# Unit 2's transposed k by a transposing transfer, its state products eight matmul rows later

## The chip, the cores and the metric

The kernel runs on one core of a Trainium2 chip. The metric is the device time of one execution in microseconds (us); the figure given for a kernel is the median of its runs. Profiles come from one profiled execution, whose times run from the start of its span.

## What is computed

Two blocks follow one another, on 4 batches of 768 tokens. The first is a gated linear recurrence in 8 heads of 48 columns, the second a normalization and a two-layer network of width 384 and 1536 with a residual:

```python
f = 1.0 / (1.0 + np.exp(-f_logit))
for t in range(S):
    state = f[:, :, t, :, None] * state + np.einsum('bhd,bhe->bhde', k[:, :, t], v[:, :, t])
    y[:, :, t] = np.einsum('bhd,bhde->bhe', q[:, :, t], state)
...
xn = (x - mu) / np.sqrt(var + 1e-06) * g_ln
ch = np.maximum(xn @ w_ch1, 0.0) @ w_ch2
return (x + ch).astype(np.float32)
```

Data type is float32 throughout.

## The kernel before

The 768 tokens are cut into 12 units of 64 tokens of all 4 batches (256 rows each). Within a unit the recurrence is done by matmuls: gates and their running products (two scans, `after` and `upto`, on VectorE) scale k and q into `kh` and `qh`; `scores` multiplies them, `causal` masks the result into `sc`, `values` multiplies it by v into `py`, and `carried` adds what the state of earlier units gives. For the state that goes on to the next unit, kh is needed with tokens across partitions: the stage `kt` makes this transposed copy, `chunk` multiplies it by v into the PSUM tile `shared` (TensorE, line 851), and `state` adds it to `kept`, the state already scaled by the unit's gates. `stats`, `norm` and `turn` prepare the result for the network (mlp), whose steps are the tokens m0, m1 and so on. `x0`, `x1` are finished output rows of units 0 and 1, the tiles `po` their second-layer products.

Nothing is scheduled by a planner: the string START writes out by hand the order of the first units, UNIT that of one later unit, and each engine executes its instructions in the order in which they are recorded. Tokens: `a2.kt` is stage kt of unit 2; `m0` a step of unit 0's network; `l4k` a load (capital L on ACT's queue); `u`, `U`, `t`, `T` mix weights on VectorE or GpSimd.

There are two ways to transpose. Units 0 to 2 use TensorE against an identity (tiles `tr`, `kp`) and copy the result out of PSUM. From unit 3 on (DIRECT = 3) a token pair such as P4k1 P4k0 first copies two halves of the 32-bit data as 16-bit planes (`split`: a ScalarE copy into a tile `planes`, of which there are three in rotation, then a DMA to DRAM, on SP's queue for a capital P and on GpSimd's for a small p), and a token such as x4k, or the stage kt, reads them back by a transposing DMA on SP's queue (`transfer`, `transposed`). The name K (tiles `Kplanes`, `Khalves`) stands for kh, small k, q and f for raw inputs.

Each DMA started by SP or ACT takes one of eight semaphores in turn, and its issuing queue waits there until the DMA that held it before has landed; in the rows of the order these are DMAHW0 to DMAHW7.

Of the kernel before, what the change touches and what calls it, by code (L numbers as in the profile page):

```python
# [306 lines left out]
h01 a1.upto w l1k h01 a1.kept f h01 h01 h00 a2.gates a1.q a1.kx a1.carried r l1v a1.k w f  # L307
a1.scores l3f a1.causal h00 r h01 a1.values a1.kt l2k f l2q w a1.stats r h01 a1.norm a1.rstd
a1.chunk P3f0 w h00 a1.turn a2.kx a2.after p3f1 a2.k r m1 m1 a2.upto f f l3k w a2.q r p3k0 x3f
a1.state m1 f a2.kept l4v P3k1 l2v m1 l3q r m1 m1 w x3k r a2.carried a3.gates w a2.scores w u U  # L310
a2.causal P3q1 m0 m0 a2.kt a3.after m0 U P3q0 L4f a2.values a3.k a2.stats L4k a2.chunk P4f1 m1
x3q m1 a2.state a3.upto p4f0 m0 l5f a2.norm U p3K1 u m0 a2.turn m0 P4k0 m1 P3K0 T a3.q x4f u u
P4k1 u a4.gates l4q u a3.kt a3.kept m2 m2 P5f0 m2 a3.carried l3v a4.after a3.scores m2 p4q0 x4k
m2 a4.upto u m2 u a3.causal p4q1 t m2 s2 a3.chunk a4.k t L5k a3.values a3.state x4q p5k0 a3.stats
m1 m1 a3.norm P5f1 P4K1 m2 U m2 a4.q x5f m2 p5k1 l6f l5q m2 a4.kept m2 a3.turn y3 l5v U m2 m1
p4K0 a5.gates
"""
UNIT = """
a{n}.kt a{n}.carried p{p}f1 a{o}.after a{n}.scores m{m} a{n}.causal m{m} m{m} m{m} P{o}q0 m{m}
# [8 lines left out]
def kernel(  # L328
# [22 lines left out]
    T = 64  # L351
# [9 lines left out]
    NU = S // T  # L361
# [3 lines left out]
    PLAIN = 2  # L365
    FIRST = 3
    DIRECT = 3
    HALVED = 1
    PIECE = 768
    R = 2  # L370
# [23 lines left out]
    def one_bank(name):  # L394
        return ps1.tile([P, 512], FP32, tag="one", name=name)
# [5 lines left out]
    for name in "fqk":  # L401
        t = consts.tile([P, G, H, 64], FP32, name=f"{name}raw")
# [11 lines left out]
    def raw_of(n, name):  # L414

        return wide_heads["k" if n >= DIRECT and name == "q" else name]

    by_gates = {}

    def split(n, name, i, queue):  # L420

        if n >= NU or n < DIRECT:
            return
        if (n, name) not in halved:
            halved[n, name] = drams.tile([P, 2, 2, 64 * H], U16, tag=f"{name}halves",
                                         name=f"{name}halves{n}")
        planes = raws.tile([P, 2, 64 * H], U16, tag="planes", bufs=3,
                           name=f"{name}planes{n}_{i}")
        if name == "K":
            src = by_gates[n].rearrange("p (i s) t -> p i (s t)", i=2)[:, i].bitcast(U16).rearrange(  # L430
                "p (c two) -> p two c", two=2)
            to, there = planes, halved[n, name][:, :, i]
        else:
            src = raw_of(n, name).rearrange("p g h e -> p (g h e)")[
                :, i * D:i * D + (H - 1) * R * D + 64]
            src = bass.AP(tensor=src.tensor, offset=src.offset,
                          ap=[src.ap[0], [R * D, H], [1, 64]]).bitcast(U16).rearrange(
                              "p h (c two) -> p two h c", two=2)
            to, there = planes.rearrange("p two (h c) -> p two h c", h=H), halved[n, name][:, i]
        nc.scalar.copy(out=to, in_=src)  # L440
        queue.dma_start(out=there, in_=planes)  # L441

    def transfer(n, name):

        if n >= NU or n < DIRECT:
            return
# [7 lines left out]
    def transposed(dst, blocks, there):  # L454
        nc.sync.dma_start_transpose(
            out=dst.bitcast(U16).rearrange("p (a r) -> p a r", a=blocks), in_=there)

    def load(n, name, gs=range(B // 2), engines=(nc.sync,)):
# [7 lines left out]
        for b in (b for b in range(B) if b // 2 in gs):  # L466
            to = loaded[n, name]
            if name == "v" or n < DIRECT:
                to = to[(b % 2) * T:(b % 2 + 1) * T, b // 2, :, 0:D]
# [166 lines left out]
    def attention(n):  # L636

        both = range(G)
        pairs, order = (by_batch, "g a") if n < DIRECT else (by_heads, "a g")
        gt = gates  # L640
# [5 lines left out]
        def new(name, shape, **kw):  # L646
            if name not in at:
                at[name] = work.tile(shape, FP32, tag=name, name=f"{name}{n}", **kw)
            return at[name]
# [35 lines left out]
        def times(dst, pts, by):  # L685
            for g, pt in pts.items():
                segs = segments([g])
                nc.vector.tensor_tensor(out=dst[:, segs], in0=pt, in1=by[:, segs, 1:E1],
                                        op=ALU.mult)

        def do_gates(gs=both):
            new("after", [P, NS, E1])
            new("upto", [P, NS, E1])
            new("total", [P, NS], bufs=2)
            if n >= DIRECT:
                nc.scalar.activation(out=gv[:, :, 1:E1], in_=turned["f"], func=AF.Sigmoid)
# [15 lines left out]
        def do_k(gs=both):  # L712
            kh = new("kh", [P, NS, T])
            if n < DIRECT:
                times(kh, {g: at["pk"][g] for g in gs}, at["after"])
            else:
                nc.vector.tensor_tensor(out=kh, in0=turned["k"], in1=at["after"][:, :, 1:E1],  # L717
                                        op=ALU.mult)
                by_gates[n] = kh

        def do_q(gs=both):
            qh = new("qh", [P, NS, T])
# [65 lines left out]
        def do_kt():  # L788

            kt, kh = new("kt", [P, GA, P]), at["kh"]  # L790
            if n >= DIRECT:
                transposed(kt.rearrange("p e c -> p (e c)"), GA,
                           halved.pop((n, "K")).rearrange("p two i c -> (p two) (i c)"))
                return
            for g in range(G):
                pt = one_bank(f"kp{n}").rearrange("p (a c) -> p a c", a=NP)
                for a in range(NP):
                    e = g * NP + a
                    nc.tensor.transpose(
                        pt[:, a], kh[:, 2 * e:2 * e + 2].rearrange("p b t -> p (b t)"), ident)  # L800
                nc.scalar.copy(out=kt[:, g * NP:(g + 1) * NP], in_=pt)
# [53 lines left out]
        def do_state():  # L855
            if n < NU - 1:
# [3 lines left out]
                else:  # L860
                    nc.scalar.copy(out=state, in_=pnv)

        stages = {"gates": do_gates, "after": do_after, "upto": do_upto, "kx": do_k_across,
                  "k": do_k, "q": do_q, "kept": do_kept, "carried": do_carried,
                  "scores": do_scores, "causal": do_causal, "kt": do_kt, "values": do_values,
                  "stats": do_stats, "rstd": do_rstd, "chunk": do_chunk, "state": do_state,
                  "norm": lambda gs=both: normalize(n, gs), "turn": lambda gs=both: turn(n, gs)}
        if n < HALVED:
            for name in ("gates", "after", "upto", "kx", "k", "q", "scores", "causal", "values",
# [5 lines left out]
    def normalize(n, gs):  # L875
        x = x_of[n]
        _, mv, rstd = norm_of[n]
        if n not in xn_of:
            xn_of[n] = work.tile([P, G, DM], FP32, tag="xn", name=f"xn{n}")
        for g in gs:  # L880
            if n < PLAIN:
                nc.vector.tensor_scalar(out=xn_of[n][:, g], in0=x[:, g], scalar1=mv[:, g, 0:1],
                                        scalar2=None, op0=ALU.subtract)
                continue
            nc.vector.tensor_scalar(out=xn_of[n][:, g], in0=x[:, g], scalar1=mv[:, g, 0:1],
                                    scalar2=rstd[:, g:g + 1], op0=ALU.subtract, op1=ALU.mult)

    def turn(n, gs):
        xn = xn_of[n]
        if n not in xt_of:  # L890
            xt_of[n] = work.tile([P, KD, W], FP32, tag="xt", bufs=2, name=f"xt{n}")
        xt = xt_of[n]
        for g in gs:
            pt = one_bank(f"xp{n}")[:, 0:KD * P].rearrange("p (m t) -> p m t", m=KD)
            for m in range(KD):
                nc.tensor.transpose(pt[:, m], xn[:, g, m * P:(m + 1) * P], ident)  # L896
            for m in range(KD):
                nc.scalar.mul(out=xt[:, m, g * P:(g + 1) * P], in_=pt[:, m],  # L898
                              mul=gain[:, m:m + 1])
# [117 lines left out]
    def mlp(n):  # L1017
# [6 lines left out]
        h = h_of[n]  # L1024
        if n < HALVED:
            pass
# [177 lines left out]
```

## Time and profile before

| | |
|---|---|
| median of 3 runs | 430.35 us (429.78 to 431.18) |
| the profiled execution's own time | 429.14 us |
| its span, first to last instruction | 427.4 us |
| TensorE matmul busy | 414.1 us, 97% of the span |
| VectorE / ScalarE / GpSimd busy | 331.6 / 214.4 / 123.4 us |
| mean granted TensorE clock | 0.988 |

The 1.74 us between own time and span lie before the first and after the last instruction. Where TensorE is busy without a break, the end is set by how much it has to do. The other engines' idle time then matters only where TensorE comes to wait for them.

### The profile page before, as it was taken

What the parts mean: (1) busy time and instruction counts of PE and PEld (TensorE: products, weight loads), DVE (VectorE), ACT (ScalarE), POOL (GpSimd) and SP (SyncE); (2) the same over time, 40 slices, a digit from 0 to 9 for tenths busy, and PEclk for the clock granted to TensorE, in tenths of its full rate; (3) what the DMA queues carried; (4) which work ended last, traced back from release to release, by engine and by line L of the source; (5) the groups of instructions that cost most, each with busy time, mean ns of one, the idle gap of its engine ahead of it and who ended that gap; (6) DMA issues with size and microseconds to landing.
All of it is one profiled execution on the core that took longest, in us unless ns stands there. A gap on an engine that the chain in (4) does not pass through costs nothing.

```text
span 427.4 us, 12961 instructions
## 1 busy us (share of the span) xinstructions
PE 414.1 (97%) x5429; PEld 386.6 (90%) x5429; DVE 331.6 (78%) x539; ACT 214.4 (50%) x364; POOL 123.4 (29%) x146
## 2 busy tenths in 40 slices
PE   6699999999999999999999999999999999999995
PEld 4589887667979999999999999999999999999995
DVE  5989896845986779879879879878879878664561
ACT  2495857452544464573574583573583453341320
POOL 2255543660033015016015016025025014012021
PEclk9599999999999999999999999999999999999999
DMA  9999999887989897886697897797695781301001
GB/s 171 286 223 183 216 281 229 190 206 182 177 121 233 164 226 207 209 192 176 166 235 186 192 220 173 184 213 201 161 221 154 178 130 50 88 2 28 13 9 34
DMA packets 167647, 71.68 MB, mean 168 GB/s; under 512 B 151760, under 2 KB 157840, under 8 KB 167584
## 3 DMA queue, kind: packets, MB, share of 16 engines
q1 hardware_dynamic: 151728, 54.38, 61.3%
q0 software_dynamic: 3872, 12.64, 8.4%
q10 hardware_dynamic: 11984, 3.79, 4.3%
q8 instruction: 44, 0.72, 0.7%
q14 instruction: 19, 0.16, 0.1%
HBM read 28.31 MB, written 23.59 MB: 121 GB/s over the span
## 4 chain that ended last, share of the span: by engine, by line
PE 90%; DVE 3%; DMA 2%; SPq 2%; ACT 2%; issue 1%; POOL 0%; ACTq 0%; DVEq 0%; POOLq 0%
PE pp L1062 32%; PE bx L961 11%; PE by L961 10%; PE po L1042 7%; PE ph L1032 7%; PE bz L961 4%; PE py L808 3%; PE py L758 3%; PE shared L772 2%; PE bw L961 2%; PE bv L961 2%; PE shared L851 2%; PE xp L896 2%; SPq L475 2%; DMA fraw<-in_f_logit_dram 1%; PE idle L577 1%
## 5 line engine op out<-in xcount | busy, mean ns | idle before, releaser
L972 ACT ACTIVATE h<-h 128x512 f32<-128x512 f32 x45 | 28.4, 631 | 44.0 <-DVE h L969 37.9
L1062 PE MATMUL pp<-mixed,h 128*128 128x192 f32 x240 | 42.4, 326 | 0.0
L1062 PE MATMUL pp<-w,h 128*128 128x192 f32 x240 | 40.8, 326 | 0.0
L1062 PE MATMUL pp<-mixed,s 128*128 128x192 f32 x240 | 40.6, 326 | 0.0
L1062 PEld LDWEIGHTS pp<-mixed,s 128*128 128x128 f32 x240 | 39.3, 190 | 0.0
L1062 PEld LDWEIGHTS pp<-w,h 128*128 128x128 f32 x240 | 38.9, 190 | 0.3
L1062 PEld LDWEIGHTS pp<-mixed,h 128*128 128x128 f32 x240 | 39.1, 190 | 0.1
L969 DVE TENSOR_TENSOR h<-h,bx 128x512 f32<-128x512 f32 x36 | 24.6, 683 | 16.9 <-PE bx L961 16.1
L898 ACT ACTIVATE xt<-xp,gain 128x128 f32<-128x128 f32 x72 | 20.0, 377 | 32.9 <-PE xp L896 32.9
L440 ACT COPY Kplanes<-kh 128x1024 uint16<-128x1024 uint16 x18 | 18.3, 1048 | 31.0 <-DVE kh L717 25.7
L441 POOL DMA_DIRECT2D qhalves<-qplanes x9 | 4.9, 548 | 97.5 <-ACT qplanes L440 97.5
L669 DVE TENSOR_TENSOR_SCAN after<-gates,ends 128x1040 f32<-128x1040 f32 (+1 forms) x13 | 28.1, 2165 | 6.2 <-ACT gates L700 3.4
L1032 PE MATMUL ph<-xt,w 128*128 128x256 f32 x144 | 31.9, 380 | 0.4 <-ACT xt L898 0.4
L1042 PE MATMUL po<-w,h 128*128 128x384 f32 x96 | 32.3, 489 | 0.0
L1032 PEld LDWEIGHTS ph<-xt,w 128*128 128x128 f32 x144 | 27.1, 190 | 4.5 <-ACT xt L898 0.6
L961 PE MATMUL bx<-y,v 128*128 128x128 f32 x216 | 28.5, 275 | 0.0
L681 DVE TENSOR_TENSOR_SCAN upto<-gates,starts 128x1040 f32<-128x1040 f32 (+1 forms) x13 | 28.1, 2158 | 0.5
L1042 PEld LDWEIGHTS po<-w,h 128*128 128x128 f32 x96 | 17.8, 190 | 11.3
L961 PEld LDWEIGHTS bx<-y,v 128*128 128x128 f32 x216 | 26.3, 192 | 0.0
L839 POOL TENSOR_SCALAR rstd<-mv 128x2 f32<-128x2 f32 x12 | 7.5, 626 | 61.4 <-DVE mv L832 61.3
L440 ACT COPY kplanes<-kraw 128x1024 uint16<-128x1024 uint16 x18 | 18.2, 1045 | 10.2 <-DMA kraw<-in_k_dram 6.7
L563 POOL TENSOR_TENSOR w<-w_0upper,w_0units 128x768 int32<-128x768 int32 x7 | 14.6, 2089 | 25.0 <-DVE w_0upper L561 20.7
(173 smaller groups left out, 961.7 us busy)
## 6 DMA issues: line engine op xcount, KB each, us to landing
w_0words<-in_moe_w_ch_dram SPq DMA_DIRECT2D x7, 768.0 KB, 6.3
v<-in_v_dram SPq DMA_DIRECT2D x46, 96.0 KB, 4.0
Khalves<-Kplanes POOLq DMA_DIRECT2D x16, 256.0 KB, 3.5
kraw<-in_k_dram SPq DMA_DIRECT2D x40, 96.0 KB, 4.1
fhalves<-fplanes POOLq DMA_DIRECT2D x14, 256.0 KB, 3.9
kraw<-in_q_dram SPq DMA_DIRECT2D x36, 96.0 KB, 3.0
fraw<-in_f_logit_dram ACTq DMA_DIRECT2D x27, 96.0 KB, 2.8
khalves<-kplanes POOLq DMA_DIRECT2D x9, 256.0 KB, 3.4
```

What stands on the lines that cost most here:

```text
L440: nc.scalar.copy(out=to, in_=src)
L563: nc.gpsimd.tensor_tensor(out=to.bitcast(I32), in0=upper, in1=units, op=ALU.add)
L669: nc.vector.tensor_tensor_scan(out=at["after"].rearrange(flat)[:, c0:c1][:, ::-1], data0=gt[:, c0 + 1:c1 + 1][:, ::-1], data1=ends.rearran ...
L681: nc.vector.tensor_tensor_scan(out=at["upto"].rearrange(flat)[:, c0:c1], data0=gt[:, c0:c1], data1=starts.rearrange(flat)[:, c0:c1], initi ...
L758: nc.tensor.matmul(py[half(b ^ r), r, e * D:(e + 1) * D], lhsT=qh[head_rows(r), 2 * e + b], rhs=kept[head_rows(r), b, e], start=e == 0, st ...
L898: nc.scalar.mul(out=xt[:, m, g * P:(g + 1) * P], in_=pt[:, m], mul=gain[:, m:m + 1])
L961: nc.tensor.matmul(banks[bank][:, i], lhsT=right[:, i * P:(i + 1) * P], rhs=left, start=new and i == 0, stop=True, skip_group_check=True)
L969: nc.vector.tensor_tensor(out=out[to], in0=out[to], in1=bank, op=op)
L972: nc.scalar.activation(out=out[to], in_=out[to] if bank is None else bank, func=AF.Relu)
L1032: nc.tensor.matmul(ph[:, j], lhsT=w1[:, m, (i + j) * P:(i + j + 1) * P], rhs=xt[:, m], start=m == 0, stop=m == KD - 1)
L1042: nc.tensor.matmul(po, lhsT=h[:, i, g * P:(g + 1) * P], rhs=w2[:, i], start=i == 0, stop=i == KF - 1)
L1062: nc.tensor.matmul(pp, lhsT=a[:, i], rhs=b[:, i], start=i == 0, stop=i == KH - 1)
```

## The change

Unit 2 takes the second way of transposing for its kh, and unit 2's stages in START are put in another order. `split` takes K from unit 2 (BACK = 2), `do_k` records kh for all units, and `do_kt` uses the transposing transfer from unit 2 on.

```diff
+    BACK = 2
...
-        if n >= NU or n < DIRECT:
+        if n >= NU or n < (BACK if name == "K" else DIRECT):
...
-                by_gates[n] = kh
+            by_gates[n] = kh
...
-            if n >= DIRECT:
+            if n >= BACK:
                 transposed(kt.rearrange("p e c -> p (e c)"), GA,
...
-a1.state m1 f a2.kept l4v P3k1 l2v m1 l3q r m1 m1 w x3k r a2.carried a3.gates w a2.scores w u U
+a1.state m1 f a2.kept l4v P3k1 l2v m1 l3q r m1 m1 w x3k r a2.carried a3.gates P2K1 P2K0 w
```

All later tokens of units 3 and up keep their order.

On TensorE, around unit 2's products (`py2`, `sc2`, `kt2` are unit 2's; `po0`, `po1` the second layer of units 0 and 1; `xp2` the turn of unit 2), before:

```order
L772 MATMUL shared_119<-qh2_866,kh2_826 64x64 x32
L1042 MATMUL po0_1057<-w2_60,h0_409 128x384 x8
L799 MATMUL kp2_1067<-ident_58,kh2_826 128x128 x4
L799 MATMUL kp2_1073<-ident_58,kh2_826 128x128 x4
L1042 MATMUL po0_1057<-w2_60,h0_409 128x384 x4
L808 MATMUL py2_958<-v2_911,sc2_1051 64x48 x32
L851 MATMUL shared_119<-v2_911,kt2_1066 48x48 x32
L1042 MATMUL po1_1182<-w2_60,h1_833 128x384 x8
L1042 MATMUL po0_1199<-w2_60,h0_409 128x384 x8
L896 MATMUL xp2_1222<-ident_58,xn2_1208 128x128 x3
```

and now:

```order
L773 MATMUL shared_119<-qh2_866,kh2_826 64x64 x32
L1043 MATMUL po0_1064<-w2_60,h0_409 128x384 x12
L809 MATMUL py2_958<-v2_911,sc2_1044 64x48 x32
L1043 MATMUL po1_1146<-w2_60,h1_833 128x384 x8
L1043 MATMUL po0_1165<-w2_60,h0_409 128x384 x4
L852 MATMUL shared_119<-v2_911,kt2_1085 48x48 x32
L1043 MATMUL po0_1165<-w2_60,h0_409 128x384 x4
L897 MATMUL xp2_1218<-ident_58,xn2_1156 128x128 x3
```

The eight transposes `kp2` are gone, and the state products (`shared<-v2,kt2`) stand behind twelve more rows of second-layer products.

On SP's queue, which starts most DMAs, before, with what each waits for:

```order
L455 DMA_TRANSPOSE qraw_88<-khalves3_884 128x4x512 [waits DMAHW0_49,DMASW1_49,PE_49]
L441 DMA qhalves3_1053<-qplanes3_1_1054 128x1024 [waits DMAHW1_49,Activation_49]
L1050 DMA out_0_dram<-x0_268 64x384 [waits DMAHW2_49,DVE_49]
L1050 DMA out_0_dram<-x0_268 64x384 [waits DMAHW3_49]
L441 DMA qhalves3_1053<-qplanes3_0_1088 128x1024 [waits DMAHW5_49,Activation_49]
L441 DMA fhalves4_1178<-fplanes4_1_1179 128x1024 [waits DMAHW5_49,Activation_49]
L455 DMA_TRANSPOSE turned_888<-qhalves3_1053 128x4x512 [waits DMAHW6_49,DMAHW1_49]
```

and now:

```order
L456 DMA_TRANSPOSE qraw_88<-khalves3_884 128x4x512 [waits DMAHW0_49,DMASW1_49,PE_49]
L442 DMA Khalves2_995<-Kplanes2_1_996 256x1x512 [waits DMAHW1_49,Activation_49]
L442 DMA Khalves2_995<-Kplanes2_0_999 256x1x512 [waits DMAHW2_49,Activation_49]
L442 DMA qhalves3_1060<-qplanes3_1_1061 128x1024 [waits DMAHW3_49,Activation_49]
L1051 DMA out_0_dram<-x0_268 64x384 [waits DMAHW4_49,DVE_49]
L1051 DMA out_0_dram<-x0_268 64x384 [waits DMAHW5_49]
L442 DMA qhalves3_1060<-qplanes3_0_1082 128x1024 [waits DMAHW7_49,Activation_49]
L456 DMA_TRANSPOSE kt2_1085<-Khalves2_995 128x8x256 [waits DMAHW2_49,DMAHW1_49,DMAHW0_49]
L442 DMA fhalves4_1142<-fplanes4_1_1143 128x1024 [waits DMAHW0_49,Activation_49]
L456 DMA_TRANSPOSE turned_888<-qhalves3_1060 128x4x512 [waits DMAHW7_49,DMAHW3_49,DMAHW1_49]
```

Two stores of K halves stand behind the transfer of unit 3's k, and the transposing transfer of kt2 behind the second q store; the store of f4 behind it waits for DMAHW0, which kt2's transfer holds.

On ScalarE, whose two 16-bit copies of unit 3's q are `qplanes3`, before:

```order
L440 COPY qplanes3_1_1054<-kraw_90 128x1024 [waits DMAHW6_49,DMAHW7_49,DMAHW5_49,DMAHW4_49]
L801 COPY kt2_1066<-kp2_1067 128x512 [waits PE_49]
L801 COPY kt2_1066<-kp2_1073 128x512 [waits PE_49]
L440 COPY qplanes3_0_1088<-kraw_90 128x1024 [waits DMASW1_49,Activation_49]
L475 DMA fraw_86<-in_f_logit_dram 32x8x96 x3
L475 DMA fraw_86<-in_f_logit_dram 32x8x96 [waits DMAHW0_49]
L817 COPY x2_1127<-py2_958 128x8x48 [waits PE_49]
```

and now:

```order
L441 COPY Kplanes2_1_996<-kh2_826 128x1024
L441 COPY Kplanes2_0_999<-kh2_826 128x1024 [waits DMASW1_49,Activation_49]
L441 COPY qplanes3_1_1061<-kraw_90 128x1024 [waits DMAHW6_49,DMAHW5_49,DMAHW7_49,DMAHW4_49,Activation_49]
L441 COPY qplanes3_0_1082<-kraw_90 128x1024 [waits DMAHW1_49,Activation_49]
L476 DMA fraw_86<-in_f_logit_dram 32x8x96 x2
L476 DMA fraw_86<-in_f_logit_dram 32x8x96 [waits DMAHW2_49]
L476 DMA fraw_86<-in_f_logit_dram 32x8x96 [waits DMAHW3_49]
L818 COPY x2_1123<-py2_958 128x8x48 [waits PE_49]
```

Two copies of K planes are new and the two copies out of `kp2` gone; the second q copy now waits for DMAHW1, the first K store, since it takes that store's tile of the three in rotation.

On VectorE `causal` of unit 2 (`sc2`) stands ahead of the first weight mix `v13`, `norm` of unit 2 (`xn2`) ahead of unit 3's scan `upto`, and `state` of unit 2 behind it.

More of the change, by code (lines that the diff above doesn't have):

```diff
@@ L309 @@
 a1.chunk P3f0 w h00 a1.turn a2.kx a2.after p3f1 a2.k r m1 m1 a2.upto f f l3k w a2.q r p3k0 x3f
-a1.state m1 f a2.kept l4v P3k1 l2v m1 l3q r m1 m1 w x3k r a2.carried a3.gates w a2.scores w u U
[L311 to L316, printed above, removed]
+a1.state m1 f a2.kept l4v P3k1 l2v m1 l3q r m1 m1 w x3k r a2.carried a3.gates P2K1 P2K0 w
+a2.scores w a2.causal u U P3q1 m0 m0 m0 a3.after U P3q0 a2.kt L4f a2.values a3.k a2.stats L4k
+P4f1 m1 x3q m1 a2.norm a3.upto p4f0 m0 a2.chunk a2.state l5f U p3K1 u m0 a2.turn m0 P4k0 m1 P3K0
+T a3.q x4f u u P4k1 u a4.gates l4q u a3.kt a3.kept m2 m2 P5f0 m2 a3.carried l3v a4.after
+a3.scores m2 p4q0 x4k m2 a4.upto u m2 u a3.causal p4q1 t m2 s2 a3.chunk a4.k t L5k a3.values
+a3.state x4q p5k0 a3.stats m1 m1 a3.norm P5f1 P4K1 m2 U m2 a4.q x5f m2 p5k1 l6f l5q m2 a4.kept m2
+a3.turn y3 l5v U m2 m1 p4K0 a5.gates
 """
```

## The prediction

> **What bounds the kernel now.** I read the page's first part, then the chain of work that ended last, then what TensorE waited for in the whole run:
>
> ```profile
> PE 414.1 (97%) x5429; PEld 386.6 (90%) x5429; DVE 331.6 (78%) x539; ACT 214.4 (50%) x364; POOL 123.4 (29%) x146
> PE 90%; DVE 3%; DMA 2%; SPq 2%; ACT 2%; issue 1%; POOL 0%; ACTq 0%; DVEq 0%; POOLq 0%
> 52.86 1.35 PE L1032 MATMUL ph<-xt,w 128*128 128x256 f32 x5 [0.38 <-ACT xt L898]
> ```
>
> TensorE is busy 97% of the span, and the chain is TensorE's for 90%. The list of TensorE's waits in the whole run has six entries, and the last in time is the 0.38 us at 52.86. The edit lies at 70 to 100 us, where TensorE has no gap, so a microsecond taken off its work there comes off the end, and a microsecond of waiting put there goes onto it. The chain around the edit (start, length, what):
>
> ```profile
> 71.57 5.36 PE po L1042 x16
> 76.93 0.87 PE kp L799 x8
> 77.80 2.58 PE po L1042 x8
> 80.38 1.08 PE py L808 x64
> 81.46 0.72 PE shared L851 x64
> 82.18 10.52 PE po L1042 x32
> 92.70 0.65 PE xp L896 x6
> 93.35 5.16 PE po L1042 x16
> ```
>
> One row of the program's order is two matmuls here (x16 for eight rows).
>
> **What goes.** The eight transposes: 0.87 us, on the path. Their two ScalarE copies (0.58 us each, the first below) are off it: worth nothing.
>
> **What the new place of the state products costs.** Sixteen second-layer matmuls take 5.16 us behind `xp`, but 5.36 behind the scores, and 32 take 10.52 behind `shared`, 0.20 over twice 5.16. So a run of full-size matmuls that follows small ones loses 0.20 us. Before there are two such runs (at 71.57 and 82.18), now three (behind scores, `py2` and `shared`): +0.20 us. The sum so far: -0.67 us.
>
> **When TensorE comes to the state products.** 71.57 + 5.36 + 2.58 = 79.51 for `py2`, + 1.08 = 80.59 for po1's eight rows, + 5.36 = 85.95 for po0's four, + 2.58 = 88.53. There it needs kt2, by then a DMA's work. When does it land? ScalarE and its queue, and SP's:
>
> ```profile
> 72.39 1.07 ACT L696 ACTIVATE gates<-turned 128x1024 f32<-128x1024 f32 x1
> 78.38 1.05 ACT L440 COPY qplanes<-kraw 128x1024 uint16<-128x1024 uint16 x1 [4.91 <-DMA kraw<-in_q_dram]
> 79.33 0.58 ACT L801 COPY kt<-kp 128x512 f32<-128x512 f32 x1
> 80.28 1.06 ACT L440 COPY qplanes<-kraw 128x1024 uint16<-128x1024 uint16 x1
> 80.92 0.32 ACTq L475 DMA_DIRECT2D fraw<-in_f_logit_dram  x1
> 81.53 0.48 ACT L817 COPY x<-py 128x384 f32<-128x384 f32 x1 [0.19 <-PE py L808]
> 82.87 3.94 ACTq L475 DMA_DIRECT2D kraw<-in_k_dram  x4
> ```
>
> ```profile
> 76.17 1.92 SPq L455 DMA_TRANSPOSE qraw<-khalves  x1
> 79.45 0.37 SPq L441 DMA_DIRECT2D qhalves<-qplanes  x1
> 82.16 2.01 SPq L1050 DMA_DIRECT2D out_dram<-x  x2
> 84.27 0.54 SPq L441 DMA_DIRECT2D qhalves<-qplanes  x1
> 88.00 0.34 SPq L441 DMA_DIRECT2D fhalves<-fplanes  x1
> 88.43 2.02 SPq L455 DMA_TRANSPOSE turned<-qhalves  x1
> ```
>
> The two K copies cost what the q copy of the same shape does, 1.05 each; they fit, from 73.5 to 75.6, into the 4.91 us in which ScalarE waits for q: cost nothing, and if the gates came over 2.8 us later they would push the q copy. The K stores cannot be issued before SP has issued k3's transposing transfer, at 76.17 + 1.92 = 78.09. Both fit before 79.45 (0.37 to 0.54 us of issue each, as the q stores): nothing on the queue.
>
> When does the first of them land? Below are the medians from issue to landing of SP's stores of K and q halves, then the nine transposing transfers into kt (least, median, most):
>
> ```profile
> Khalves<-Kplanes SPq DMA_DIRECT2D x2, 256.0 KB, 4.0
> qhalves<-qplanes SPq DMA_DIRECT2D x9, 256.0 KB, 3.2
> L455 SPq DMA_TRANSPOSE kt<-Khalves x9: 1354/1900/3170, 106.2 to 368.1; - x9
> DMA to landing us min/median/max: 4.4/5.1/6.2
> ```
>
> With the 4.0 of the K stores, 78.1 + 4.0 = 82.1. It agrees with the queue: the fourth f load waited for k3's transfer to land and went at 80.92, and the K store's bytes follow that transfer. The second q copy, at 80.28 before, now waits for that landing in its tile: 82.1, + 1.06 = 83.2; its store goes out behind it (+0.5), and the transfer of kt2 at about 83.7. The output x0 ahead of it is ready earlier, as po0 now ends at 79.51 instead of 80.38.
>
> From issue to landing I have 4.4 as the least, 5.1 as the median and 6.2 as the most among its kind, and below all this 7.5 for q3's transfer at 88.43, which stands in the same place. The load on the DMA engines decides:
>
> ```profile
> 78.00:82.00 4.00, 4.00 (x136) 2.79 (x134) 4.00 (x4) 3.43 (x5) 3.83 (x2) 1.00 1.11 231
> 82.00:86.00 4.00, 4.00 (x29) 2.44 (x19) 3.93 (x8) 0.96 (x3) 1.39 (x3) 1.00 0.68 182
> 86.00:90.00 4.00, 4.00 (x14) 2.32 (x13) 3.39 (x5) 2.94 (x3) 1.00 (x3) 1.00 0.56 146
> 106.00:110.00 4.00, 4.00 (x138) 3.54 (x137) 3.12 (x4) 3.16 (x5) 0.00 (x0) 1.00 0.94 195
> kt<-Khalves SPq DMA_TRANSPOSE x1, 6.2
> turned<-qhalves SPq DMA_TRANSPOSE x1, 7.5
> ```
>
> The last column but one is the DMA share. From 82 to 90 us it is 0.62 in the mean; half a megabyte of K stores and another half for the transfer come on top, and at the rates shown (182 and 231 GB/s) one megabyte is some 5 us of all engines, so these 8 us become full. The transfer of kt3, issued at 106.19 into a share of 0.94, took 6.2: nearest in kind, time and load, so I take it. Landing: 83.7 + 6.2 = 89.9, and TensorE, ready at 88.53, waits 1.37 us. The sum: -0.87 + 0.20 + 1.37 = **+0.70 us**.
>
> The Trainium skill ("Advanced Engine Details and Errata", section X-Bar Transpose (TRN2)) says that transposing DMAs are as fast as regular ones, 350 to 400 GB/s. An estimate from it: the transfer moves 256 KB more than a q store, 0.7 us, which with the store's 3.2 gives 3.9, so kt2 at 87.6 and no wait, a sum of -0.67. This trace does not agree: no transfer into kt took under 4.4 us.
>
> **What the rest costs.** Each is covered:
>
> ```profile
> 78.01 1.22 DVE L778 TENSOR_TENSOR sc<-shared,causal 128x1024 f32<-128x1024 f32 x1
> 88.62 0.85 DVE L885 TENSOR_SCALAR xn<-x,mv,rstd 128x384 f32<-128x384 f32 x2
> 99.09 1.22 DVE L726 TENSOR_TENSOR qh<-turned,upto 128x1024 f32<-128x1024 f32 x1
> 102.97 1.02 DVE L743 TENSOR_TENSOR kept<-state,total 128x384 f32<-128x384 f32 x2
> 106.22 1.15 PE L758 MATMUL py<-kept,qh 48*64 48x48 f32 x64
> ```
>
> `causal` in its old place would end at 79.23 against `py2` at 79.51, so moving it ahead of the mix is worth nothing but safety. Behind the second q copy ScalarE's queue holds the four f loads, the last two of which wait for a K and a q store; I put the copies of `py2` to x2 about 2.5 us later than 81.53, statistics with them. `norm`, no longer behind the 2.3 us scan, keeps its place near 88.6 and `xp2`, now at about 93, stays covered by some 4 us. The f4 store and q3's transfer on SP wait for kt2's landing: 88.43 becomes about 90.5. With 7.5 us it lands at 98, ahead of its reader at 99.09, and from that reader's chain (`kept` ends at 103.99) to `carried` at 106.22 another 2.2 us are free. `state` behind `upto` ends near 93.5, ten microseconds ahead of `kept`. So the only step that can reach TensorE is kt2.
>
> **Rivals.** (B) kt2 lands before TensorE is there, issued at 83.7 and 4.4 us long (88.1), or a little quicker before: then the clean -0.67 us is left. For it: the edit leaves 5 us from issue to use, and the kind's median of 5.1 waits only 0.3. Against it: the least values come from later units, with a lighter queue. The skill's rate above would lead here.
>
> (C) The other side: kt2 is held up as q3's transfer was, 7.5 us: 91.2, a wait of 2.7 us, sum +2.0 us. It is the same queue with ACT's four f and four k loads moved into the transfer's time, which the late second q copy brings about. It decides from a landing at 90.5 on. For it: the share and the row of 7.5. Against it: GpSimd's two stores that competed with q3's transfer come only after kt2, since ScalarE makes their planes later. The Trainium skill ("DMA: Bandwidth & Descriptors", section Queues, rings and completion order) says that each DMA engine takes turns between the queues that have work, so that ACT's loads would hold up SP's transfer; no run here shows the two apart.
>
> (D) The change does nothing: excluded, the transposes leave TensorE.
>
> **How the numbers follow.** 0.45 for a landing between 89 and 90.5 (my forecast), 0.20 for B, 0.30 for C, 0.05 for something unseen. The profiled execution has 429.14 us, its span 427.4 and 1.74 around it; with +0.70 it becomes 429.84. The median of the runs is 1.21 above the profiled one, so the forecast is 430.35 + 0.7, rounded to 431.0. B gives 429.7, C 432.4; with the spread of the runs (429.78 to 431.18) the range is 429.4 to 432.8. About 0.3%, 1.3 us, is what a measurement can tell from no change. The forecast and B lie within it, C beyond 1.3 us lies outside; even the whole 0.87 us is under it on the fast side. So faster 0.06, same 0.62, slower 0.32.
>
> **What would show it.** In the changed kernel's profile: no `kp` after 60 us; `py2` near 79.5; the second q copy near 82; kt2's transfer issued near 83.7; the matmuls `shared<-v2,kt2` idle ahead by 0.5 to 2 us, put down to a DMA; `xp2` and `carried` of unit 3 without a wait. If those matmuls have no gap, B holds and the time is below 430. If the gap is over 2 us, C holds. A wait at `carried` of unit 3, or in the weight mixes, would mean that I covered the wrong step.

## The result, and the profile after

| | before | after |
|---|---|---|
| median of 9 runs each, us (least, most) | 431.25 (429.78, 432.81) | 440.01 (434.39, 445.54) |
| profiled execution, us (span) | 429.14 (427.4) | 437.84 (436.1) |
| mean granted clock of TensorE | 0.988 | 0.984 |
| unit 3's `carried` begins on the chain, us | 106.29 | 110.88 |
| last VectorE piece of the chain (L1070, L1071) begins, us | 423.07 | 431.46 |

The change made the kernel slower: the ratio is 1.0126, 95% interval 1.0077 to 1.0174. That ratio leaves out executions over 1.5% above the kernel's own fastest, and the changed kernel scatters more than that by itself; run once more beside other kernels (below) it stood at 1.0268 (1.0223 to 1.0314). The last row of the table is the end of TensorE's work. What lies behind it is 4.3 us before and 4.6 after, but up to 6.4 in some kernels below, with and without the change, so I compare kernels by this row where a microsecond matters.

The page's first part, then the chain's shares, of the kernel after:

```profile
PE 414.6 (95%) x5421; PEld 386.5 (89%) x5421; DVE 332.8 (76%) x539; ACT 215.4 (49%) x364; POOL 121.8 (28%) x146
PE 84%; DMA 6%; SPq 3%; DVE 2%; ACT 2%; issue 2%; POOL 0%; ACTq 0%; DVEq 0%; POOLq 0%
```

TensorE has eight matmuls fewer and is no less busy. Its share of the chain fell from 90% to 84%, and DMA and "issue" took it over. The list of its waits (waiting line, releaser: us in total, times, longest) shows two entries that are new:

```profile
PE by L962 <- issue: 3.7, 2, 2.0
PE shared L852 <- DMA kt<-Khalves: 3.5, 1, 3.5
```

The second of them, seen on the chain around the edit (start, length, what):

```profile
81.62 1.05 ACT qplanes L441
83.55 8.58 DMA kt<-Khalves
92.17 1.53 PE shared L852 x64
93.70 3.58 PE po L1043 x8
97.94 5.16 PE po L1043 x16
103.11 7.77 PE ph L1033 x36
110.88 1.08 PE py L759 x64
```

The transfer of kt2 took 8.58 us, and TensorE, ready at 88.68, stood still for 3.48. Then `shared` took 1.53 us and the eight `po` matmuls behind it 3.58; in kernels of this order that have no wait there (e6 and e12 below) they take 0.86 and 2.78. The windows tell why; the last columns are PEclk, DMA share and GB/s:

```profile
91.00:92.00 1.00, 0.00 (x0) 0.00 (x0) 1.00 (x1) 1.00 (x2) 0.00 (x0) 0.94 0.01 0
92.00:93.00 1.00, 0.83 (x40) 0.83 (x44) 0.59 (x1) 1.00 (x2) 0.56 (x1) 0.50 0.00 0
93.00:94.00 1.00, 1.00 (x37) 0.91 (x30) 0.23 (x1) 0.10 (x1) 0.97 (x2) 0.50 0.90 262
94.00:95.00 1.00, 1.00 (x2) 0.47 (x2) 1.00 (x2) 0.00 (x0) 1.00 (x3) 0.50 0.96 264
95.00:96.00 1.00, 1.00 (x4) 0.66 (x3) 0.42 (x1) 0.00 (x0) 1.00 (x2) 0.85 1.18 249
```

After the wait the granted clock was one half for 3.4 us, from 91.9 to 95.3. The sum around the edit: -0.87 (transposes) + 0.34 (the new place of the state products, see e6) + 3.48 (wait) + 0.67 + 0.80 (half clock, in `shared` and `po`) = 4.42. Measured, the stretch from the start of unit 2's `carried` to that of unit 3's is 41.18 us instead of 36.74, so 4.44 longer. `carried` of unit 3 begins 4.59 later than before; the other 0.15 us was there ahead of the edit's place. The clock rule of the Trainium skill ("TensorE: Matmul & The Clock Gate", section Why this matters for your kernels) says that TensorE should not stand idle for over about 3 us between matmuls, since one idle window brings the clock back to half; this wait agrees.

The first of the two entries lies a hundred microseconds later and does not touch the edit:

```profile
190.90 1.08 PE py L809 x64
191.98 0.72 PE shared L852 x64
192.70 2.02 issue
194.72 1.05 PE by L962 x8
```

"issue" means that no semaphore held TensorE. The other such gap is 1.68 us at 291.27. They are 4801 and 7617 recorded TensorE instructions into the program, 11 times 256 apart. The queue q8 of the page carries instructions, 44 packets for the run, 16,384 bytes each in the trace. In the answers on the DMA traffic (queue, kind: packets, MB, share) the stretch from 179.8 to 192.3 has no such packet, and the one from 192.3 to 194.8 has:

```profile
q1 hardware_dynamic: 855, 0.28, 47.7%
q0 software_dynamic: 81, 0.26, 32.5%
q8 instruction: 1, 0.02, 2.2%
```

So a block of instructions arrived just as TensorE had run out. The count of the packets agrees: the first gap ends with the 18th packet of q8, the second with the 29th, and 11 packets for 11 times 256 instructions are 256 a packet. TensorE went on 1.4 us after each of the two had landed. In the kernel before, the 18th packet ran from 184.5 to 185.4 us, 2.5 us before TensorE came to instruction 4801 at 187.8, and there is no gap; the answer for its stretch from 180 to 185:

```profile
q8 instruction: 1, 0.02, 1.1%
```

Of 8.39 us in the chain's end, 4.44 come from the edit's place, 3.70 from these two gaps, and 0.15 was there before the edit's place.

### The profile page after: what moved, and what is told of

It reads as the page before. It is cut to its first block, busy times and chain, and to the rows that moved or that the text cites. A ratio compares the mean times of both kernels' runs of the same rounds, so it can differ in the third digit from the quotient of the medians.

```text
span 436.1 us, 12951 instructions
## 1 busy us (share of the span) xinstructions
PE 414.6 (95%) x5421; PEld 386.5 (89%) x5421; DVE 332.8 (76%) x539; ACT 215.4 (49%) x364; POOL 121.8 (28%) x146
## 4 chain that ended last, share of the span: by engine, by line
PE 84%; DMA 6%; SPq 3%; DVE 2%; ACT 2%; issue 2%; POOL 0%; ACTq 0%; DVEq 0%; POOLq 0%
PE pp L1063 31%; PE bx L962 11%; PE by L962 10%; PE po L1043 4%; PE bz L962 4%; PE ph L1033 4%; PE ph L911 3%; PE py L809 3%; PE py L759 2%; PE shared L773 2%; PE bw L962 2%; DMA kt<-Khalves 2%; PE shared L852 2%; PE bv L962 2%; SPq L476 2%
## 5 line engine op out<-in xcount | busy, mean ns | idle before, releaser
L441 ACT COPY Kplanes<-kh 128x1024 uint16<-128x1024 uint16 x20 | 20.2, 1050 | 31.5 <-DVE kh L718 26.6
L1043 PE MATMUL po<-w,h 128*128 128x384 f32 x96 | 33.2, 500 | 0.0
L962 PE MATMUL by<-y,v 128*128 128x128 f32 x144 | 20.0, 281 | 3.7 <-issue 3.7
```

Of the source, the lines that this page charges most:

```text
L962: nc.tensor.matmul(banks[bank][:, i], lhsT=right[:, i * P:(i + 1) * P], rhs=left, start=new and i == 0, stop=True, skip_group_check=True)
L1043: nc.tensor.matmul(po, lhsT=h[:, i, g * P:(g + 1) * P], rhs=w2[:, i], start=i == 0, stop=i == KF - 1)
```

## The experiments

Four theories are named in what was expected. W: the loss near 90 us is the wait for kt2 plus half clock. Q: the transfer is slow because ScalarE's queue shares the DMA engines. F: the late gaps are TensorE's instruction fetch, placed by the number of instructions ahead. R: they follow from the stall near 90 us. The kernels ran in three sets (e1 to e4, e5 to e8, e9 to e12), each beside the kernel before, whose medians were 430.85, 430.22 and 430.97. "d" is one idle matmul, four recorded TensorE instructions.

| kernel | median us | ratio to before (95%) | wait at `shared` of unit 2 | late gaps | `carried` 3 | last VectorE piece |
|---|---|---|---|---|---|---|
| before | 431.25 | | none | none | 106.29 | 423.07 |
| e1_moves_only | 431.30 | 1.0026 (0.9989-1.0063) | none | none | 107.52 | 424.27 |
| e2_pad | 435.21 | 1.0132 (1.0072-1.0192) | 2.76 | none | 108.89 | 425.66 |
| e3_loads_sp | 434.81 | 1.0107 (1.0070-1.0143) | 0.33 | 1.65, 0.86 | 106.52 | 425.93 |
| e4_early | 433.40 | 1.0089 (1.0050-1.0129) | none | 1.33, 1.13 | 106.53 | 426.41 |
| e5_before_less | 437.45 | 1.0170 (1.0131-1.0210) | none | 1.42, 1.10 | 109.92 | 429.54 |
| e6_early_pad | 430.19 | 1.0001 (0.9979-1.0023) | none | none | 106.48 | 423.52 |
| e7_early_pad_f | 430.39 | 1.0007 (0.9984-1.0030) | none | none | 106.04 | 422.94 |
| e8_after_again | 441.06 | 1.0268 (1.0223-1.0314) | 2.99 | 1.44, 1.09 | 111.98 | 431.39 |
| e9_fill | 437.55 | 1.0101 (1.0046-1.0156) | 3.59 | none | 112.45 | 429.21 |
| e10_before_m8 | 431.95 | 1.0028 (0.9997-1.0060) | none | 1.08 (second) | 107.60 | 425.54 |
| e11_before_p16 | 430.76 | 0.9994 (0.9963-1.0025) | none | none | 107.40 | 424.72 |
| e12_later_chunk | 431.44 | 1.0010 (0.9977-1.0043) | none | none | 106.90 | 423.70 |

### The moves without the transfer

```diff
-    BACK = 2
+    BACK = 3
```

> The changed order of START with unit 2's kh still transposed by TensorE (BACK = 3), so no transfer, and as many TensorE instructions as before. The changed kernel's profile shows three things: a wait of 3.5 us for kt2, half the clock for 3.4 us behind it, and two gaps of about 2 us at 194.7 and 293.0 us for which no releaser is shown. Theory W (the loss near 90 us is the wait and the clock behind it) expects no gap at the state products and unit 3's carried products at 106.2 as before, within 0.5. Theory F (the two late gaps come from fetching TensorE's instructions, at a place set by how many instructions stand ahead) expects no late gap, since the count is that of before. Rival R (the late gaps follow from the stall near 90 us, by whatever it shifted) expects none either. All three: a time within 1 us of before. If the moves of mask, norm and state products themselves cost, it is slower by more.

1.0026, an interval that holds 1: moving `causal`, `norm` and the state products costs nothing that the measurement can tell. The eight transposes are back, and with them no wait and no late gap. In the profile the moves cost 0.34 us: 37.08 from unit 2's `carried` to unit 3's, instead of 36.74. The rest of the 1.2 us by which `carried` of unit 3 is behind that of before was there at unit 2's `carried` (70.44 against 69.55), and 0.59 of it is an early gap put down to "issue", at 41.70 us and instruction 961. In the list of its waits:

```profile
PE shared L773 <- issue: 0.6, 1, 0.6
```

Up to there TensorE's instructions are those of the kernel before, whose profile has no gap at this place: the number of instructions alone does not decide whether one opens.

### The change with the instructions counted back

```diff
-l0q1 a0.after1 f a0.kx1 ... a0.q1 r f
+l0q1 a0.after1 f d d a0.kx1 ... a0.q1 r f d d
```

> The changed kernel with four idle matmuls (16 TensorE instructions, in two places of the first 18 us where TensorE waits anyway), which puts all later TensorE instructions back to their old count but one. Theory F expects the wait for kt2 unchanged (3.5 us, half clock behind it), but no gap of 1.5 us or more after 120 us: about 434.5 us, and little spread. Rival R expects the late gaps as in the changed kernel, 437 us or more with a spread of several us.

Four idle matmuls at the start, where TensorE waits for loads, and both late gaps are gone. The wait for kt2 was 2.76 us this time (the transfer took 7.9), and in the windows the clock stayed whole:

```profile
91.00:92.00 1.00, 0.41 (x35) 0.42 (x39) 1.00 (x1) 1.00 (x3) 0.00 (x0) 1.00 0.00 0
92.00:93.00 1.00, 1.00 (x50) 0.81 (x39) 1.00 (x2) 1.00 (x2) 0.61 (x1) 1.00 0.57 193
```

So the wait without half clock cost little more than its length: the stretch between the two `carried` is 2.29 us longer than before, the wait less the 0.5 us that the change saves without one (e6). The timed runs, for which F had expected little spread, lie between 432.14 and 438.23, all but the profiled one above 434; which of them had a longer transfer or half clock is not to be seen in a time alone.

### ScalarE's loads on SyncE's queue

```diff
-... P3q0 a2.kt L4f a2.values a3.k a2.stats L4k
+... P3q0 a2.kt l4f a2.values a3.k a2.stats l4k
```

> The changed kernel with unit 4's eight loads of f and k on SP's queue, behind the transfer of kt2, instead of on ScalarE's beside it; all else as changed. Theory Q (the transfer took 8.6 us instead of some 5 because ScalarE's queue took 47% of the DMA work meanwhile) expects it to land within 5 to 6 us of its issue, near 89, a gap at the state products under 1 us, no half clock, and unit 3's carried products near 106. Rival (the transfer is slow because the stores ahead of it in its own queue are, or because a transfer is slow behind another) expects 7 us or more and the gap to stay. For the late gaps: theory F expects them as in the changed kernel, since TensorE's instructions are the same in number and place, 2 to 5 us in all; rival R expects none.

The rows of the DMA traffic from kt2's issue to its landing, first of the kernel after (84 to 92.2), then of this one (84 to 89.2):

```profile
q1 hardware_dynamic: 2228, 0.78, 52.6%
q10 hardware_dynamic: 1921, 0.69, 47.4%
kraw<-in_k_dram ACTq DMA_DIRECT2D x4, 96.0 KB, 5.5
kt<-Khalves SPq DMA_TRANSPOSE x1, 8.6
```

```profile
q1 hardware_dynamic: 2806, 1.09, 86.1%
fraw<-in_f_logit_dram SPq DMA_DIRECT2D x4, 96.0 KB, 3.2
kt<-Khalves SPq DMA_TRANSPOSE x1, 4.5
```

With the loads on the same queue, in line with the transfer, it took 4.5 instead of 8.6 us, and the wait was 0.33. Q holds. In the five profiles in which the loads and the transfer stand where the change has them, it took 7.9 to 9.5. The late gaps stayed, without a stall near 90 us: that speaks for F and against R. With the wait mended, the kernel still is 1.1% slower than before.

### The transfer begun earlier

```diff
-... w x3k r a2.carried a3.gates P2K1 P2K0 w
-a2.scores ... U P3q0 a2.kt L4f
+... w r P2K1 a2.carried a3.gates P2K0 x3k a2.kt w
+a2.scores ... U P3q0 L4f
```

> The changed kernel with the K stores ahead of k3's transfer on SP's queue and kt2's transfer directly behind that one, some 3 us earlier and before the eight loads of ScalarE's queue. Theory W and Q expect the landing by 86, no gap at the state products (TensorE is there at 88.6), and carried products of unit 3 at 105.6, 0.7 before the 106.2 of before. Theory F expects the late gaps still, as TensorE's instructions are those of the changed kernel: 431 to 435 us. Rival R expects no late gap: about 429.7 to 430.5 us.

kt2's transfer was issued at 81.65, 1.9 us earlier, and was over before TensorE came, though at 87.74 and not by 86:

```profile
81.65 6.09 DMA kt<-Khalves
```

ScalarE's queue had a share of 12.8% of the DMA engines in this time, against 47.4% in the changed kernel. There is no wait at the state products. `carried` of unit 3 comes 0.2 us later than before and not at 105.6, as TensorE waited 0.96 us at unit 2's `xp` for a ScalarE copy. The late gaps are there again, at the same two instructions. This kernel shows them nearly by themselves: 1.0089, its median 2.6 us above that of before.

### The kernel before with 16 instructions fewer

```diff
-l0q0 L0f1 d d a0.carried d a0.gates0 d a0.after0 l0k0
+l0q0 L0f1 a0.carried a0.gates0 a0.after0 l0k0
```

> The kernel before, with four of its idle matmuls taken out at the very start (16 TensorE instructions fewer, while TensorE waits for the first loads; nothing else differs, and the output is the reference's). Theory F (the late gaps are TensorE's instruction fetch, placed by the number of instructions ahead): with 10,924 instead of 10,940 recorded instructions the block boundaries stand as in the kernel after, and the two gaps of 1 to 2 us appear near 190 and 288 us at instructions 4801 and 7617 or within a few of them; median 1.5 to 4 us above the kernel before run beside it (432.5 to 435). Theory R (the gaps follow from the change's own stall near 90 us): no such gap, since no wait of the change is in it; median within 1.3 us of before, save what the colder start costs (up to 1 us).

Nothing of the change is in this kernel, and the late gaps are there, at instructions 4801 and 7617 like those of the change. Of its chain, the first three pieces put down to "issue", among others:

```profile
41.99 1.55 issue
44.10 4.50 PE ph L910 x24
191.75 1.42 issue
289.82 1.10 issue
```

For the late gaps F is shown and R excluded: four idle matmuls less at the start are enough. The first gap stands at instruction 961, 15 times 256 ahead of 4801, and ends with the 3rd packet of q8, 15 ahead of the 18th. Half clock follows it, though TensorE stood still for only 1.55 us:

```profile
44.00:45.00 1.00, 1.00 (x9) 0.97 (x6) 0.85 (x1) 0.00 (x0) 1.00 (x1) 0.66 1.03 321
45.00:46.00 1.00, 1.00 (x7) 1.00 (x6) 0.38 (x1) 0.00 (x0) 0.59 (x1) 0.50 1.39 225
46.00:47.00 1.00, 1.00 (x7) 1.00 (x7) 0.00 (x0) 0.24 (x1) 0.00 (x0) 0.50 1.16 170
47.00:48.00 1.00, 1.00 (x8) 1.00 (x8) 0.03 (x1) 1.00 (x3) 0.00 (x0) 0.63 1.10 152
```

That explains the loss beyond what I expected: 3.6 us are lost by `carried` of unit 3 (109.92 against 106.29), all of it ahead of unit 2's, and 2.5 in the late gaps. Of the 3.6, the gap is 1.55, and the 24 `ph` matmuls behind it took 4.50 us instead of the 2.88 of e1. By the rule of the Trainium skill on the clock ("TensorE: Matmul & The Clock Gate", the section named above) a gap under 3 us should not have done it; the measurement decides, and what the clock goes by stays open.

### Both mended

On top of the transfer begun earlier:

```diff
-l0q1 a0.after1 f a0.kx1 ... a0.q1 r f
+l0q1 a0.after1 f d d a0.kx1 ... a0.q1 r f d d
```

> The kernel after with unit 2's k planes and its transfer begun earlier (as in the run before with that order) and four idle matmuls more at the start, which bring TensorE's instructions back to 10,939. F: no late gap, and no wait at the state products, so 1.2 + 1.2 us less than the same order without the idles: span near 428.5, median 430 to 431.5. R: no late gap either, since it has no stall at the state products, but the order without the idles had none and showed the gaps, so R expects them here again (2.4 us in two gaps, median near 433.4).

No wait, no gap, 1.0001 (0.9979 to 1.0023). The chain around the edit is that of the plan; the first and the last line are the `carried` of units 2 and 3:

```profile
70.27 1.08 PE py L759 x64
80.23 1.08 PE py L809 x64
81.31 7.94 PE po L1043 x24
89.25 0.86 PE shared L852 x64
90.11 2.78 PE po L1043 x8
106.48 1.08 PE py L759 x64
```

R, which wanted the gaps back here, failed once more. `shared` takes 0.86 and the eight matmuls behind it 2.78 us even without a wait, against 0.72 and 2.58: a transition from full-size to small matmuls and back costs 0.34 us here, more than the 0.20 of my sum. So the clean saving is 0.87 - 0.34 = 0.53 us and not 0.67, and it is there: from one `carried` to the other are 36.21 us here, and the same in e7 and e12, against 36.74 before.

```diff
-P4f1 m1 x3q m1 a2.norm
+m1 x3q P4f1 m1 a2.norm
```

> The previous kernel with ScalarE's copy of unit 4's second f piece (P4f1) begun after the q products of unit 3 (x3q) instead of before them. In the early order without idles the transposes of unit 2's norm waited 0.96 us for that copy; if the copy's place is the cause, the wait falls under 0.4 us, and unit 3's carried stage begins near 105.7 instead of 106.5; median 0.5 to 1 us under the previous kernel, so 429.3 to 430.8. If the wait is for the load behind the copy, it stays and nothing changes (within 0.5 us).

`carried` of unit 3 begins at 106.04, the earliest of all, but the previous kernel had already lost the 0.96 us wait of e4 at unit 2's `xp`, so there was little left to mend: 1.0007 (0.9984 to 1.0030). Of the saving of 0.53 us, 0.25 is left at `carried` of unit 3, as that of unit 2 began 0.28 later than before, and 0.13 at the end of the chain; timed, it is neither shown nor excluded.

### The change again

> The changed kernel again, unaltered, beside the others. W and F: wait at the state products of unit 2 2.5 to 3.7 us, half clock behind it where the wait passes some 3 us, and the two late gaps again at instructions 4801 and 7617, 1 to 2 us each; median 436 to 441, 1.2 to 2% above before. R: late gaps only where the wait near 90 us is long.

All as in the first profile, except that the wait is shorter (2.99) and the half clock longer (91.1 to 98.0, 6.8 us). Its transfer took 9.08 us, and the eight `po` behind `shared` 5.13:

```profile
82.61 9.08 DMA kt<-Khalves
91.73 1.53 PE shared L852 x64
93.26 5.13 PE po L1043 x8
```

So the price of one and the same wait varies: against the 0.86 and 2.78 us of the clean order, half clock cost 0.67 + 0.80 = 1.47 us in the first profile, 0.67 + 2.35 = 3.02 here, and nothing after e2's 2.76 us. With these the sum comes out once more: -0.87 + 0.34 + 2.99 + 3.02 = 5.48, and the stretch between the two `carried` is 5.48 us longer than before.

### Idle matmuls in the wait

```diff
-... p4f0 m0 a2.chunk a2.state
+... p4f0 m0 d d d a2.chunk a2.state
```

(and one at the start)

> The kernel after with three idle matmuls put right before unit 2's state products, where TensorE waits for kt2, and one at the start (16 instructions in all, so the count is that of before within two). W (loss near 90 us = the wait, plus half clock because TensorE stands still): the idles keep TensorE busy for some 1.3 to 2.6 us of the 3 us, the rest of the wait falls under 2 us, the clock stays at 1.00 through 90 to 100 us, unit 3's carried stage begins some 2.5 us behind before's 106.22 instead of 4.6 to 5.7; F: no late gaps; together span 429.5 to 431.5, median 432 to 434. If the half clock does not come from standing still, the clock falls to half all the same and the median is 434 to 436.

A miss. The idles ran as planned, up to 89.96, but kt2 came still later than in the changed kernel's own profiles, and TensorE stood still for 3.59 us behind them:

```profile
83.95 9.55 DMA kt<-Khalves
93.55 1.27 PE shared L852 x64
94.81 4.05 PE po L1043 x8
```

The clock fell to half for 3.4 us again, so the test does not tell whether filling the wait would hold it. The late gaps are gone, as F says. With a transfer between 7.9 and 9.5 us, its timed runs spread from 432.56 to 442.22, and the change's own spread of 11 us has the same look; that the transfer's length is what spreads them is likely, not shown, since a timed run has no trace. Half clock seems to have a part in it, as the mean granted clock falls from 0.985 in the run of 432.56 us to 0.980 in that of 438.69.

### Where the edge of the gaps lies

```diff
-l0q0 L0f1 d d a0.carried d a0.gates0 d a0.after0 l0k0
+l0q0 L0f1 d d a0.carried a0.gates0 a0.after0 l0k0
```

> The kernel before with two of the early idle matmuls left out (8 TensorE instructions fewer). F says only that the count decides, not where the edge lies between 0 and 16 fewer: either both late gaps of 1 to 2 us are there at instructions 4801 and 7617 (median 432.5 to 435), or none (median within 1.3 us of before). R: none.

Neither of the two: with 8 instructions fewer only the second late gap is there, and the chain has it:

```profile
285.41 1.08 issue
```

In time it hardly shows (1.0028, 0.9997 to 1.0060). With 16 more than before:

```diff
-l0q1 a0.after1 f a0.kx1 ... a0.q1 r f
+l0q1 a0.after1 f d d a0.kx1 ... a0.q1 r f d d
```

> The kernel before with four idle matmuls more, at the two places where the padded kernels had them (16 TensorE instructions more). F: the block boundaries move by 16 against the program, so gaps may go or come elsewhere; those of before are none, and if none come, the median is within 1 us of before, or up to 1 us under it by the warmer clock at the start (0.93 against 0.80 in the first 25 us in the padded run). If the idles themselves are what repaired the earlier kernels and not the count, this kernel is faster than before by 1 us or more.

No late gap and no gain: 0.9994 (0.9963 to 1.0025). So the idles themselves make nothing faster; what they mended in e2 and e6 was the count.

### The state products behind the transfer

```diff
-... p4f0 m0 a2.chunk a2.state l5f U p3K1 u m0 a2.turn m0 P4k0
+... p4f0 m0 l5f U p3K1 u m0 a2.turn m0 a2.chunk a2.state P4k0
```

(with the four idle matmuls of the second experiment)

> The kernel after with four idle matmuls at the start (count as before) and unit 2's state products some 4.5 us later in TensorE's order: behind the norm's transposes and eight output matmuls instead of ahead of them. The transfer stays where the change has it and takes its 6 to 8 us. W: TensorE reaches the state products near 93.5, behind kt2's landing near 91.5, so no wait over 0.5 us, clock 1.00 there, carried of unit 3 near 106; F: no late gaps; span 427.5 to 429, median 429.5 to 431. If the transfer costs time in another way than by the wait, the median stays above 432.

The state products stand behind sixteen `po` matmuls and `xp` more (2.58 + 0.65 + 2.58 = 5.8 us). The transfer took 8.5 us from 85.3, and TensorE did not wait for it:

```profile
92.25 0.65 PE xp L897 x6
92.90 2.58 PE po L1043 x8
95.48 0.86 PE shared L852 x64
96.35 2.78 PE po L1043 x8
```

1.0010 (0.9977 to 1.0043). W is shown from the other side: the slow transfer costs only by the wait (and the clock behind it). None of the mended kernels is faster than before by more than the measurement can tell.

## Why the prediction was wrong

- **What goes, -0.87: right.** `py2` began at 79.60 (forecast 79.51), and TensorE came to the state products at 88.68 (88.53). They stand twelve rows of second-layer products later, as the sum had it, and not the eight of the title.
- **The new place of the state products, +0.20: right in kind, too small.** It is 0.34, since `shared` itself is slower behind full-size matmuls, 0.86 instead of 0.72 (e6, e12).
- **The issue of the transfer: right.** 83.55 against 83.7; the second q copy at 81.62 against 82.1.
- **"Landing: 83.7 + 6.2 = 89.9": the first step that failed.** It landed 8.58 us after its issue, and the wait was 3.48 instead of 1.37. I took the row of kt3 as nearest in kind and load; the row of the same place, q3's 7.5, was rival C's. What decided was not the share of the DMA engines in all but that ScalarE's queue was served beside SyncE's: 4.5 us with one queue, 7.9 to 9.5 with two. C had named this cause, ScalarE's eight loads in the transfer's time, and by the prediction's own sign, a gap over 2 us, C is what happened. Its wait of 2.7 us is near the 2.76 of e2, but short of the 3.48.
- **A term that the sum did not have: the clock.** I charged a wait by its length. The half clock behind it added 1.47 us in the first profile, 3.02 in the second.
- **"The only step that can reach TensorE is kt2": wrong.** Seventeen recorded instructions fewer (eight transposes with their weight loads, and one semaphore) moved the program against its instruction blocks, and two gaps of 3.7 us in all opened a hundred and two hundred microseconds later. That term had no rival; it does not come from the transfer, as the kernel before with sixteen instructions fewer shows it too.
- **The rest, covered: right.** No wait at `xp2`, at `carried` of unit 3 or in the mixes.

In the terms of the sum: forecast -0.87 + 0.20 + 1.37 = +0.70; the first profile gave -0.87 + 0.34 + 3.48 + 1.47 + 3.70 = 8.12, of 8.39 in the end of the chain, of which 0.15 lie ahead of the edit's place.

## What to carry to other kernels

Ask of a transfer that is put in front of a consumer which other queue moves bytes in those microseconds, and leave the consumer room for twice its usual time: here a place 5.8 us later in TensorE's order cost nothing that shows. Charge a wait on a busy TensorE of about 3 us more than its length, since half clock can follow. In a long unrolled program look for "issue" gaps that come after an edit in places that it does not touch, and before judging the edit bring the number of instructions ahead of them back, for instance by idle matmuls where TensorE waits anyway.

## What the runs showed that I had not expected

- A late instruction block costs TensorE 0.9 to 2.0 us a time, at the same two recorded instructions in four kernels (one of them without the change), and 16 or 17 instructions decide over it; 8 fewer gave one gap, 16 more none. Shorter gaps of the same kind stand early, at instruction 961 in e1 (0.59) and e10 (0.61) and at 1217 in e11 (0.48) and e12 (0.55); all these places are 193 past a multiple of 256. What sets the time at which a block is fetched no run here shows. The Trainium skill ("Runtime: NRT & Kernel Launch", section Instruction fetch mechanics) says that instructions come in blocks of 256, the next one fetched while the current one runs, and that this is mostly hidden; here it mostly was, and for 3.7 us of the changed kernel it was not.
- The clock halved after waits of 2.99, 3.48 and 3.59 us, not after one of 2.76, and yet after a gap of 1.55 in e5. Early in the program it halved after a wait of 1.96 us in e6, and not after one of 2.62 in e10. In these cases it stayed at one half for 3.4 or 6.8 us.
- The stretch behind the last matmul work lasts between 4.3 and 6.4 us from one profile to the next, whatever the kernel: two microseconds by which single executions differ without cause in the edit.
